# Exponential and sine tables in alternating order, exponent matmuls as row-tile pairs, constants as immediates

**Chip, cores, metric.** One Trainium2 chip, one core. The metric is the device time of one execution of the whole program in microseconds (us); medians over several runs are given. All runs told here are of the fast state.

## The reference

The program computes two independent things and sets them side by side: a segmented attention with memory (A) and a long convolution whose kernel K is a sum of complex exponentials (B). Only the making of K is touched here:

```python
dt = exp(log_dt)[:, None]
A, Bc, Cc = A_re + 1j*A_im, B_re + 1j*B_im, C_re + 1j*C_im
P = exp((dt*A)[:, :, None] * arange(L))          # D=1024, N=128, L=2048
K = einsum('dn,dnl,dn->dl', Cc, P, dt*Bc).real
...                                              # y = u convolved with K, by FFT
```

## The kernel before

B comes first, then A. B has a setup, then sixteen rounds that make tables of powers for K, then the spectra and inverse transforms. While the rounds run, A's projections of x ("pro"), the forward transforms of u ("ups", called the side matmuls here), and copies of weights are slipped in between. A itself, from 880 us on, streams weights from memory.

A round (sb) makes eight pairs of exponent matmuls (e = 0 to 7). TensorE writes the logarithm of the modulus (pa) and the angle in turns (pt); ScalarE (ACT) makes exp of the one (E) and rounds the other (kM); VectorE (DVE) takes the rounded turns off (nr); ACT makes sines (sn) and cosines (cs) of nr; DVE multiplies them by E; in the next round TensorE contracts them ("part", tile kp). Each engine takes up its work in the order of the program; the timeline under a_odd shows what that can cost, a wait of 3.20 us behind work of another kind.

```python
def exponents(pars, e):                       # four full-array matmuls, 128x328 each
    pa = ps_e.tile(...); pt = ps_t.tile(...)  # ps_e has one buffer, ps_t two
    for t_, q, Rs in ((pa, 0, (RG, RF)), (pt, 1, (RG, RN))):
        for f, R in enumerate(Rs):
            pe.matmul(t_[:, f, 0:8*NJ], lhsT=pars[q][:, e, :], rhs=R[...], start=True, stop=True)
    return pa, pt

for sb in range(17):
    npars = load_par(sb + 1)                  # four DMAs from GpSimd's queue
    for e in range(8):
        pa, pt = ex
        sc.activation(out=Es[..e], in_=pa, func=ACT.Exp)
        sc.activation(out=kM, in_=pt, func=ACT.Identity, bias=magic[:])
        v.scalar_tensor_tensor(out=nrs[..e], in0=kM, scalar=MAGIC, in1=pt, ...)
        ex = exponents(pars, e + 1)           # or of the next round
        if e == 0: v.tensor_tensor(out=ocs[1], in0=oE[1], in1=ocs[1], op=mult)
        if e % 2 == 1: part(osb, e // 2, ocs, osn)     # kp: 32 small matmuls + a DVE copy
        if e % 2 == 0: step_side()                     # ups: 8 matmuls + ACT copy or two DVE sums
    for i in range(2):
        sc.activation(out=sn[i], in_=nrs[i], func=ACT.Sin, scale=-TWO_PI)
        next(pro)
        v.tensor_scalar(nrs[i] = abs)
    next(pro)
    for i in range(2):
        sc.activation(out=cs[i], in_=nrs[i], func=ACT.Sin, scale=-TWO_PI, bias=hp[:])
        v.tensor_tensor(out=sn[i], in0=Es[i], in1=sn[i], op=mult)
        next(pro)
    v.tensor_tensor(out=cs[0], in0=Es[0], in1=cs[0], op=mult)
    next(pro); next(pro); next(mb)            # ... cut
```

kp and ups share two PSUM buffers in turn; what is still to be taken out of the older one is taken out when the next is asked for.

## Time and profile before

| | before |
|---|---|
| median, lowest, highest (first three runs) | 2541.84, 2531.63, 2552.6 us |
| profiled execution | 2562.5 us, mean clock 0.942 |
| the rounds | some 86 to 560 us |
| one round (mean of 14) | 29.0 us |

The lines behind this stand in the prediction. Read them so: an engine's busy share over the whole span says nothing about this change, since A takes two thirds of the time and is bound by DMA. What counts is one round, and in it who waits for whom.

### The profile page before, as it was taken

To read this page: it belongs to the slowest core of one execution; us is meant where nothing else is said; L and a number is where in the kernel's file an instruction comes from. 1 tells how busy PE (TensorE), PEld (TensorE's weight loads), DVE (VectorE), ACT (ScalarE), POOL (GpSimd) and SP (SyncE) were. 2 spreads that over 40 slices of the span, in tenths; PEclk is the share of its full clock that TensorE was granted. 3 is DMA by queue.
4 is the path that set the end of the run, shared out by engine and by line. 5 is a ranking of instruction groups with operands and counts; after the bars stand their busy time and mean duration, and the time that the engine had idled before them with its cause. 6 is when DMAs were issued, how large, how long until landed. Compare 5 with 4: busy or idle time off the path is not lost.

```text
span 2562.5 us, 76703 instructions
## 1 busy us (share of the span) xinstructions
PE 2055.3 (80%) x32856; PEld 1101.7 (43%) x32902; DVE 1498.0 (58%) x3224; ACT 1023.9 (40%) x1550; POOL 311.6 (12%) x601
## 2 busy tenths in 40 slices
PE   1588888857697778888888888888888888888879
PEld 1355555633242334444444444444444444444444
DVE  9687777879985245545454554545455454545450
ACT  6788788961121223323333332323333232333321
POOL 2133424442001100000000000000000000000020
PEclk6799999978898889999999999999999999999999
DMA  5665756543346999999999999999999999999992
GB/s 135 174 190 155 229 173 176 149 146 116 125 132 212 339 382 379 378 380 365 386 362 381 372 386 369 362 373 369 390 383 384 380 364 374 369 370 373 374 384 74
DMA packets 382387, 763.18 MB, mean 298 GB/s; under 512 B 118678, under 2 KB 210806, under 8 KB 379998
## 3 DMA queue, kind: packets, MB, share of 16 engines
q1 hardware_dynamic: 363006, 700.44, 76.1%
q0 software_dynamic: 14128, 39.99, 4.6%
q10 hardware_dynamic: 4912, 17.84, 2.0%
q8 instruction: 257, 4.21, 0.6%
q14 instruction: 84, 0.69, 0.1%
HBM read 703.35 MB, written 67.88 MB: 301 GB/s over the span
## 4 chain that ended last, share of the span: by engine, by line
DMA 33%; PE 28%; DVE 17%; ACT 9%; issue 8%; SPq 1%; POOL 0%; ACTq 0%; DVEq 0%; POOLq 0%
DMA wst<-WD_k 16%; PE acc L330 12%; DMA wst<-WD_o 10%; PE pp L429 3%; DMA wst<-WD_v 3%; PE pe L552 2%; ACT sn L1019 2%; PE pro L151 2%; PE tr L341 2%; ACT kM L994 1%; DVE piece L269 1%; PE ups L850 1%; ACT E L991 1%; PE pro L138 1%; ACT ev L336 1%
## 5 line engine op out<-in xcount | busy, mean ns | idle before, releaser
L330 PEld LDWEIGHTS <-hT 128*32 128x32 bf16 x12352 | 326.8, 97 | 474.1 <-issue 256.0
L330 PE MATMUL acc<-wst,hT 128*32 128x512 bf16 x3072 | 313.6, 393 | 163.3 <-DMA wst<-WD_k 67.4
L336 ACT CAST ev<-acc 128x512 bf16<-128x512 f32 x384 | 225.1, 586 | 414.4 <-PE acc L330 409.4
L429 PEld LDWEIGHTS <-oT 128*32 128x32 bf16 x8192 | 204.5, 97 | 116.6 <-issue 90.4
L269 DVE TENSOR_SCALAR piece<-keep 128x256 int32<-128x256 int32 (+1 forms) x640 | 191.4, 363 | 56.5 <-PE pp L429 31.1
L429 PE MATMUL pp<-W_o,oT 128*32 128x256 bf16 x5120 | 212.5, 277 | 6.8 <-DMA W_o<-in_A_Wo_dram 6.8
L330 PE MATMUL acc<-W_v,hT 128*32 128x512 bf16 x3072 | 211.1, 379 | 0.3 <-DMA W_v<-in_A_Wv_dram 0.3
L368 DVE TENSOR_REDUCE mx<-sc 128x8 f32<-128x320 f32 x128 | 62.4, 487 | 251.8 <-PE sc L361 251.6
L330 PE MATMUL acc<-W,hT 128*32 128x512 bf16 x2560 | 205.7, 392 | 0.0
L342 DVE COPY KT<-tr 128x512 bf16<-128x512 bf16 x64 | 27.2, 425 | 264.3 <-PE tr L341 264.3
L429 PE MATMUL pp<-wst,oT 128*32 128x256 bf16 x2560 | 129.2, 278 | 39.3 <-DMA wst<-WD_o 30.3
L342 ACT COPY QT<-tr 128x512 bf16<-128x512 bf16 x128 | 75.0, 586 | 192.6 <-PE tr L341 191.7
L1159 PE MATMUL yp<-Bt,mi 128*128 128x512 bf16 x379 | 115.5, 411 | 41.5 <-DMA mi<-MId 32.2
L416 ACT CAST oT<-pv 128x512 bf16<-128x512 f32 x128 | 75.1, 586 | 169.3 <-PE pv L402 166.9
L349 POOL COPY KT<-pk 128x128 bf16<-128x128 bf16 x128 | 37.6, 293 | 816.0 <-PE sc L361 454.4
L330 PE MATMUL acc<-W_q,hT 128*32 128x512 bf16 x1792 | 135.1, 383 | 0.0
L995 DVE SCALAR_TENSOR_TENSOR nr<-kM,ptt 128x656 f32<-128x656 f32 x128 | 104.9, 833 | 44.3 <-ACT kM L994 44.1
L151 PE MATMUL pro<-xTl,wsl 128*128 128x512 bf16 x493 | 116.6, 384 | 12.7 <-DVE kst L155 7.5
L370 ACT ACTIVATE sc<-sc 128x320 f32<-128x320 f32 x128 | 54.0, 422 | 154.8 <-DVE sc L369 148.0
L330 PE MATMUL acc<-W_k,hT 128*32 128x512 bf16 x1536 | 112.6, 401 | 0.0
L303 POOL COPY hT<-xt 128x192 bf16<-128x192 bf16 x64 | 22.2, 347 | 728.1 <-DMA xt<-XTd 442.0
L1075 PE MATMUL hps<-KT,MF 128*128 128x512 bf16 x374 | 93.3, 395 | 19.9 <-DVE x L1088 19.4
(288 smaller groups left out, 3766.7 us busy)
## 6 DMA issues: line engine op xcount, KB each, us to landing
wst<-WD_o SPq DMA_DIRECT2D x320, 512.0 KB
wst<-WD_k SPq DMA_DIRECT2D x256, 512.0 KB
wst<-WD_q SPq DMA_DIRECT2D x256, 512.0 KB
wst<-WD_v SPq DMA_DIRECT2D x256, 512.0 KB
Ud<-ux POOLq DMA_DIRECT2D x16, 1024.0 KB, 4.8
uq<-Ud SPq DMA_DIRECT2D x32, 512.0 KB
pk<-PKd SPq DMA_DIRECT2D x64, 192.0 KB
wsl<-in_A_Wk_dram SPq DMA_DIRECT2D x16, 512.0 KB
```

The lines of the kernel that those rows point to most:

```text
L151: nc.tensor.matmul(a[:], lhsT=w[:, kc, 128 * j:128 * j + 128], rhs=xTl[:, kc, :, :].rearrange("p s k -> p (s k)"), start=(kc == 0), stop=( ...
L269: nc.vector.tensor_scalar(out=out.bitcast(I32), in0=in_.bitcast(I32), scalar1=0, scalar2=None, op0=ALU.bitwise_or)
L330: nc.tensor.matmul(a[32 * g:32 * g + 32, o_:o_ + rhs.shape[1]], lhsT=hT[:, kc, :], rhs=rhs, start=(kc == 0), stop=(kc == KC - 1), tile_pos ...
L336: nc.scalar.copy(out=q[:], in_=a[:])
L342: eng(out=dst, in_=p[:, i, :, :, :])
L368: nc.vector.tensor_reduce(out=mx[:], in_=sc, axis=AX.X, op=ALU.max)
L370: nc.scalar.activation(out=sc, in_=sc, func=ACT.Exp, scale=scale)
L416: nc.scalar.copy(out=o[:], in_=p[:].rearrange("p a (g q) -> p a g q", g=4))
L429: nc.tensor.matmul(po[32 * qt:32 * qt + 32, :], lhsT=oT[:, h % 4, (h % 16) // 4, :], rhs=columns(w, 1024 * hh + 256 * qt, 256)[0][1], star ...
L995: v.scalar_tensor_tensor(out=nrs[e // 4][:, e % 4].rearrange("p f t j -> p f (t j)"), in0=kM[:], scalar=MAGIC, in1=ptv, op0=ALU.subtract, ...
L1075: pe.matmul(ps[:], lhsT=MF[:, 4 * rr + mc, cs, 128 * kc:128 * kc + 128], rhs=rhs, start=(i == 0 and mc == 0), stop=(i == 1 and mc == 3))
L1159: pe.matmul(yp[:], lhsT=m_[:, cs, kc, :], rhs=Bt[:, kc, half, j, c_, :], start=(n == 0), stop=(n == 15))
```

## The change

Its intent: Exp and Sin lie in different tables of ACT, so a round needs two table loads. If even rounds end with exponentials and odd rounds begin with them, half of the loads go. The exponent matmuls have two disjoint halves of rows, so two of them fit in the array at once as row tiles; for it the parameters are loaded twice, to both halves of the partitions. Constants pi/2 and MAGIC are given as immediates.

```diff
-def exponents(pars, e): ... four full-array matmuls
+    def rows_of(t_, par, R, e):
+        for f in range(2):
+            p = slice(64 * f, 64 * f + 64)
+            pe.matmul(t_[:, f, 0:8 * NJ], lhsT=par[p, e, :], rhs=R[p]..., start=True, stop=True, tile_position=(64 * f, 0))
+    def angles(pars, e):                      # ps_t
+    def exponents(pars, e, late_=False):      # ps_e, or ps_t in even rounds
-            for h in range(2):
-                gp.dma_start(out=par_t[sb % 2][q][24 * h:24 * h + 24],
+            for h, p0 in ((0, 0), (1, 24), (0, 64), (1, 88)):
+                gp.dma_start(out=par_t[sb % 2][q][p0:p0 + 24],
-  bias=hp[:] / bias=magic[:]
+  bias=HALF_PI / bias=MAGIC
 ...
+    for sb in range(0, 16, 2):
+        for e in range(8):                    # EVEN round: angles alone
+            fold(e, nrs, pt)                  # kM on ACT, nr on DVE
+            if e < 7: pt = angles(pars, e + 1)
+            if e == 0 and old is not None: scale(old[2], Es, 1)
+            if e % 2 == 1: old_part(e // 2)
+            if e % 2 == 0: step_side()
+        sines, with five of the round's seven projections
+        for e in range(8):                    # exponentials alone
+            power(e, Es, pa)
+            if e < 7: pa = exponents(pars, e + 1, True)
+            if e == 3: scale(sn, Es, 0); scale(cs, Es, 0)
+            if e in (2, 5): more()            # the other two projections
+        scale(sn, Es, 1); scale(cs, Es, 1)
+        sb += 1
+        for e in range(8):                    # ODD round: both, as before
+            power(e, Es, pa); fold(e, nrs, pt)
+            pa, pt = exponents(pars, e + 1), angles(pars, e + 1)
+            if e in (2, 4, 6, 7): old_part(...)        # before: e = 1, 3, 5, 7
+            if e % 2 == 0 ...: step_side()
+        sines as before, with all seven projections
```

More of the change, by code (lines that the diff above doesn't have):

```diff
@@ L597, in part_b @@
     make_identity(nc, ident[:])
-    hp = const.tile([128, 1], F32, name="hp")
-    v.memset(hp[:], HALF_PI)
-    magic = const.tile([128, 1], F32, name="magic")
-    v.memset(magic[:], MAGIC)
     ahead.open(ahead.ctx)
@@ L608, in part_b @@
     tabs = ctx1.enter_context(tc.tile_pool(name="b_tab", bufs=1))
-    RG = tabs.tile([128, 8, NJ], BF16, name="RG")
-    RF = tabs.tile([128, 8, NJ], BF16, name="RF")
-    RN = tabs.tile([128, 8, NJ], BF16, name="RN")
+    RE = tabs.tile([128, 8, NJ], BF16, name="RE")
+    RA = tabs.tile([128, 8, NJ], BF16, name="RA")
     par_t = [[tabs.tile([128, 8, 128], BF16, name="pt%d%d" % (q, n_)) for q in range(2)] for n_ in range(2)]
@@ L675, in matrices @@
                     v.tensor_scalar(out=tm[:].bitcast(I32), in0=tm[:].bitcast(I32), scalar1=0x7FFFFFFF, scalar2=None, op0=ALU.bitwise_and)
-                    sc.activation(out=MF[:, c - 4:c - 2, 0, :], in_=tm[:], func=ACT.Sin, scale=-TWO_PI, bias=hp[:])
+                    sc.activation(out=MF[:, c - 4:c - 2, 0, :], in_=tm[:], func=ACT.Sin, scale=-TWO_PI, bias=HALF_PI)
                 if 2 <= c < 18:
@@ L685, in matrices @@
                     kMs[c] = mg.tile([128, 2, 512], F32, name="mkM", tag="mkM")
-                    sc.activation(out=kMs[c][:], in_=tms[c][:], func=ACT.Identity, bias=magic[:])
+                    sc.activation(out=kMs[c][:], in_=tms[c][:], func=ACT.Identity, bias=MAGIC)
                 yield
@@ L707, in part_b @@
         pI = par.tile([128, 3], I32, name="pI")
-        gp.iota(pI[:, 0:1], pattern=[[1, 1]], base=0, channel_multiplier=1)
+        gp.iota(pI[:, 2:3], pattern=[[1, 1]], base=0, channel_multiplier=1)
+        v.tensor_scalar(out=pI[:, 0:1], in0=pI[:, 2:3], scalar1=63, scalar2=None, op0=ALU.bitwise_and)
         v.tensor_scalar(out=pI[:, 1:2], in0=pI[:, 0:1], scalar1=3, scalar2=None, op0=ALU.bitwise_and)
@@ L727, in part_b @@
         v.tensor_scalar(out=jF[:, 1, :], in0=jF[:, 1, :], scalar1=low[:], scalar2=pF[:, 2:3], op0=ALU.mult, op1=ALU.add)
-        for i, R in ((0, RG), (1, RF)):
-            v.tensor_tensor(out=R[:], in0=bcast_mid(own[:], NJ), in1=bcast_front(jF[:, i, :], 8), op=ALU.mult)
-        v.tensor_scalar(out=RN[:], in0=RF[:], scalar1=-1.0, scalar2=None, op0=ALU.mult)
+        v.tensor_copy(out=jF[0:64, 1, :], in_=jF[0:64, 0, :])
+        v.tensor_tensor(out=RE[:], in0=bcast_mid(own[:], NJ), in1=bcast_front(jF[:, 1, :], 8), op=ALU.mult)
+        v.tensor_copy(out=RA[0:64], in_=RE[0:64])
+        v.tensor_scalar(out=RA[64:128], in0=RE[64:128], scalar1=-1.0, scalar2=None, op0=ALU.mult)
         for ts in par_t:
@@ L924, in put_values @@
             put(Kd[640:641, dsl], kx[P0:P0 + 1, 40, :])
-    def exponents(pars, e):
-        pa = ps_e.tile([128, 2, 512], F32, name="pa", tag="pa")
-        pt = ps_t.tile([128, 2, 512], F32, name="ptt", tag="ptt")
-        for t_, q, Rs in ((pa, 0, (RG, RF)), (pt, 1, (RG, RN))):
-            for f, R in enumerate(Rs):
-                pe.matmul(t_[:, f, 0:8 * NJ], lhsT=pars[q][:, e, :], rhs=R[:].rearrange("p a b -> p (a b)"), start=True, stop=True)
-        return pa, pt
+    def rows_of(t_, par, R, e):
+        for f in range(2):
+            p = slice(64 * f, 64 * f + 64)
+            pe.matmul(t_[:, f, 0:8 * NJ], lhsT=par[p, e, :], rhs=R[p].rearrange("p a b -> p (a b)"), start=True, stop=True, tile_position=(64 * f, 0))
+        return t_
+    def angles(pars, e):
+        return rows_of(ps_t.tile([128, 2, 512], F32, name="ptt", tag="ptt"), pars[1], RA, e)
+    def exponents(pars, e, late_=False):
+        pool, tag = (ps_t, "ptt") if late_ else (ps_e, "pa")
+        return rows_of(pool.tile([128, 2, 512], F32, name="pa", tag=tag), pars[0], RE, e)
     def load_k(dh, qs, KT):
@@ L971, in load_u, with fold, power @@
         return us
+    flat = "p f t j -> p f (t j)"
+    def fold(e, nrs, pt):
+        ptv = pt[:, :, 0:8 * NJ]
+        kM = tmp.tile([128, 2, 8 * NJ], F32, name="kM", tag="kM")
+        sc.activation(out=kM[:], in_=ptv, func=ACT.Identity, bias=MAGIC)
+        v.scalar_tensor_tensor(out=nrs[e // 4][:, e % 4].rearrange(flat), in0=kM[:], scalar=MAGIC, in1=ptv, op0=ALU.subtract, op1=ALU.subtract)
+    def power(e, Es, pa):
+        sc.activation(out=Es[e // 4][:, e % 4], in_=pa[:, :, 0:8 * NJ].rearrange("p f (t j) -> p f t j", t=8), func=ACT.Exp)
@@ new lines, in scale, with sines @@
+    def scale(x, E, i):
+        v.tensor_tensor(out=x[i][:], in0=E[i][:], in1=x[i][:], op=ALU.mult)
+    def sines(nrs, sn, cs, after):
+        for i in range(2):
+            sc.activation(out=sn[i][:], in_=nrs[i][:], func=ACT.Sin, scale=-TWO_PI)
+            after()
+            v.tensor_scalar(out=nrs[i][:].bitcast(I32), in0=nrs[i][:].bitcast(I32), scalar1=0x7FFFFFFF, scalar2=None, op0=ALU.bitwise_and)
+        after()
+        for i in range(2):
+            sc.activation(out=cs[i][:], in_=nrs[i][:], func=ACT.Sin, scale=-TWO_PI, bias=HALF_PI)
+            yield i
+            after()
@@ L975, in part_b, with small_steps, shift_late, old_part @@
+    def small_steps():
+        next(mb, None)
+        for _ in range(2):
+            if copies:
+                copies.pop(0)()
+    def shift_late():
+        if late:
+            late.pop(0)()
+    def old_part(k):
+        if old is not None:
+            osb, osn, ocs = old
+            part(osb, k, ocs, osn)
+            if k == 3 and osb % 4 == 3:
+                put_values(osb)
+    def more(n=1):
+        for _ in range(n):
+            next(pro, None)
     pars = load_par(0)
     old = None
-    ex = exponents(pars, 0)
@@ L978, in part_b @@
-    for sb in range(17):
+    pt = angles(pars, 0)
+    for sb in range(0, 16, 2):
+        nrs = [tmp.tile(shg, F32, name="nr", tag="nr%d" % i, bufs=1) for i in range(2)]
+        npars = load_par(sb + 1)
+        for e in range(8):
+            fold(e, nrs, pt)
+            if e < 7:
+                pt = angles(pars, e + 1)
+            if e == 0 and old is not None:
+                scale(old[2], Es, 1)
+            if e % 2 == 1:
+                old_part(e // 2)
+            shift_late()
+            if e % 2 == 0:
+                step_side()
+        sn = [tmp.tile(shg, BF16, name="sn", tag="sn%d" % i, bufs=1) for i in range(2)]
+        cs = [tmp.tile(shg, BF16, name="cs", tag="cs%d" % i, bufs=1) for i in range(2)]
+        for i in sines(nrs, sn, cs, more):
+            pass
+        pa = exponents(pars, 0, True)
+        small_steps()
+        Es = [tmp.tile(shg, BF16, name="E", tag="E%d" % i, bufs=1) for i in range(2)]
+        for e in range(8):
+            power(e, Es, pa)
+            if e < 7:
+                pa = exponents(pars, e + 1, True)
+            if e == 3:
+                scale(sn, Es, 0)
+                scale(cs, Es, 0)
+            if e in (2, 5):
+                more()
+        pars = npars
+        pa, pt = exponents(pars, 0), angles(pars, 0)
+        scale(sn, Es, 1)
+        scale(cs, Es, 1)
+        old = (sb, sn, cs)
+        sb += 1
@@ L983, in part_b @@
             ks = [load_k(0, (sy,), ahead.pool.tile([128, 16, DH], BF16, name="KT", tag="kst"))]
-        if sb < 16:
-            nrs = [tmp.tile(shg, F32, name="nr", tag="nr%d" % i, bufs=1) for i in range(2)]
-            Es = [tmp.tile(shg, BF16, name="E", tag="E%d" % i, bufs=1) for i in range(2)]
+        nrs = [tmp.tile(shg, F32, name="nr", tag="nr%d" % i, bufs=1) for i in range(2)]
+        Es = [tmp.tile(shg, BF16, name="E", tag="E%d" % i, bufs=1) for i in range(2)]
         npars = load_par(sb + 1) if sb < 15 else None
         for e in range(8):
-            if sb < 16:
-                pa, pt = ex
-                sc.activation(out=Es[e // 4][:, e % 4], in_=pa[:, :, 0:8 * NJ].rearrange("p f (t j) -> p f t j", t=8), func=ACT.Exp)
-                ptv = pt[:, :, 0:8 * NJ]
-                kM = tmp.tile([128, 2, 8 * NJ], F32, name="kM", tag="kM")
-                sc.activation(out=kM[:], in_=ptv, func=ACT.Identity, bias=magic[:])
-                v.scalar_tensor_tensor(out=nrs[e // 4][:, e % 4].rearrange("p f t j -> p f (t j)"), in0=kM[:], scalar=MAGIC, in1=ptv,
-                                       op0=ALU.subtract, op1=ALU.subtract)
-                if e < 7:
-                    ex = exponents(pars, e + 1)
-                elif sb < 15:
-                    ex = exponents(npars, 0)
-            if old is not None:
-                osb, oE, osn, ocs = old
-                if e == 0:
-                    v.tensor_tensor(out=ocs[1][:], in0=oE[1][:], in1=ocs[1][:], op=ALU.mult)
-                if e % 2 == 1:
-                    part(osb, e // 2, ocs, osn)
-                if e == 7 and osb % 4 == 3:
-                    put_values(osb)
-            if late:
-                late.pop(0)()
+            power(e, Es, pa)
+            fold(e, nrs, pt)
+            if e < 7:
+                pa, pt = exponents(pars, e + 1), angles(pars, e + 1)
+            elif sb < 15:
+                pt = angles(npars, 0)
+            if e in (2, 4, 6, 7):
+                old_part(min(e // 2 - 1, 2) if e < 7 else 3)
+            shift_late()
             if e % 2 == 0 or (e == 7 and sb % 4 == 1):
                 step_side()
-        if sb == 16:
-            break
         pars = npars
@@ L1017, in part_b @@
         cs = [tmp.tile(shg, BF16, name="cs", tag="cs%d" % i, bufs=1) for i in range(2)]
-        for i in range(2):
-            sc.activation(out=sn[i][:], in_=nrs[i][:], func=ACT.Sin, scale=-TWO_PI)
-            next(pro, None)
-            v.tensor_scalar(out=nrs[i][:].bitcast(I32), in0=nrs[i][:].bitcast(I32), scalar1=0x7FFFFFFF, scalar2=None, op0=ALU.bitwise_and)
-        next(pro, None)
-        for i in range(2):
-            sc.activation(out=cs[i][:], in_=nrs[i][:], func=ACT.Sin, scale=-TWO_PI, bias=hp[:])
-            v.tensor_tensor(out=sn[i][:], in0=Es[i][:], in1=sn[i][:], op=ALU.mult)
-            next(pro, None)
-        v.tensor_tensor(out=cs[0][:], in0=Es[0][:], in1=cs[0][:], op=ALU.mult)
-        next(pro, None)
-        next(pro, None)
-        next(mb, None)
-        for _ in range(2):
-            if copies:
-                copies.pop(0)()
-        old = (sb, Es, sn, cs)
+        for i in sines(nrs, sn, cs, more):
+            scale(sn, Es, i)
+        scale(cs, Es, 0)
+        more(2)
+        small_steps()
+        old = (sb, sn, cs)
+    scale(old[2], Es, 1)
+    for k in range(4):
+        old_part(k)
+        shift_late()
+        step_side()
     for n_, f_ in enumerate(late):
```

## The prediction

> **What bounds the kernel now.** I read the page's slices first, then the sums by stretch of time, then the groups of the tables' stretch, then its chain, then one round's timeline.
>
> From the page: the busy tenths in 40 slices of 64 us each.
>
> ```profile
> PE   1588888857697778888888888888888888888879
> ...
> ACT  6788788961121223323333332323333232333321
> ...
> DMA  5665756543346999999999999999999999999992
> ```
>
> ACT is high only in the first nine slices, which hold the setup and the tables (from 86 us to some 560 us). From slice 14 on the DMA engines are full, and the chain there is weight transfers. The change touches only the first stretch, so whatever it wins or loses is a shift of some 475 us out of 2542.
>
> Sums by stretch, one for the fourteen rounds from the second to the fifteenth (the rounds begin at the load of the exponentials' table), columns in order length, PE, PEld, DVE, ACT, POOL, clock, DMA:
>
> ```profile
> 119.17:524.79 405.62, 339.07 (x3765) 225.06 (x3782) 316.14 (x383) 351.86 (x367) 159.89 (x229) 0.95 0.65 184
> ```
>
> A round is 405.62/14 = 29.0 us. ACT works 351.86/14 = 25.1 of it (87%), PE 24.2 and DVE 22.6. No engine is full; three nearly full ones hand work to each other in strict order. The groups of that stretch on ACT (busy us, mean ns, then idle before and its releasers):
>
> ```profile
> L994 ACT ACTIVATE kM<-ptt,magic 128x656 f32<-128x656 f32 x112 | 91.0, 812 | 0.4 <-PE ptt L931 0.4
> L991 ACT ACTIVATE E<-pa 128x656 bf16<-128x656 f32 x112 | 80.8, 722 | 13.2 <-PE pa L931 9.8 <-DVE cs L1027 1.9
> L1024 ACT ACTIVATE cs<-nr,hp 128x2624 bf16<-128x2624 f32 x28 | 68.4, 2477 | 0.2 <-DVE nr L1021 0.2
> L1019 ACT ACTIVATE sn<-nr 128x2624 bf16<-128x2624 f32 x28 | 66.1, 2387 | 0.2
> L991 ACT ACT_TABLE_LOAD x15 | 19.2, 1283 | 0.3
> L1019 ACT ACT_TABLE_LOAD x14 | 18.0, 1283 | 0.2
> L855 ACT COPY ua<-ups 128x512 f32<-128x512 f32 x28 | 16.5, 588 | 18.1 <-PE ups L850 18.1
> L155 ACT CAST kst<-pro 128x512 bf16<-128x512 f32 x18 | 10.4, 576 | 12.5 <-PE pro L151 12.5
> L143 ACT CAST vst<-pro 128x512 bf16<-128x512 f32 x12 | 7.0, 580 | 8.7 <-PE pro L138 8.7
> ```
>
> Every round loads two tables, 2.57 us, and ACT's idle time, 53.8 us or 3.84 a round, is nearly all waits for PE: side matmuls (ups), projections (pro), exponents (pa). The chain of this stretch says the same: it changes hands all the time, no engine has half of it.
>
> ```profile
> by line: ACT sn L1019 11.0%; PE pro L151 10.6%; issue 10.2%; ACT kM L994 7.1%; PE ups L850 6.8%; PE pro L138 6.2%; ACT E L991 6.2%; DVE nr L995 5.8%; DVE us L859 3.6%; DVE us L858 3.4%; DVE nr L1021 3.2%; ACT L991 2.8%; DVE cs L1004 2.8%; D
> ```
>
> **What the Trainium skill says.** (1) "ScalarE: Activation LUTs", section "What ACT_TABLE_LOAD costs": a switch is a load of about 1283 ns plus a drain of about 1380 ns. The trace agrees on the load, 1283 ns each time; the drain isn't there to save: at 254.12 the load begins 0.02 us after the copy before it, and the sine at 255.41 follows it at once. I count 1.283 us a load. (2) The same section: a per-partition pointer operand adds about 93 ns to an ACTIVATE. The trace agrees: the cosines with hp take 2477 ns, the sines without it 2387, 90 ns apart. (3) "TensorE: Matmul & The Clock Gate", section "The mechanism" of Part 3: matmuls in different row groups start some 4 ns apart and run together. No run of this kernel shows it, since it has no row tiles. (4) "TensorEngine Tiling (Array Packing)", section "Key Properties": changing the tiling mode drains TensorE. The trace agrees roughly: in the timeline of PE, exponent matmuls start 0.14 us apart, but the first column-tiled kp matmul starts 0.23 us after the last of them (250.21 to 250.44), so a switch costs about 0.09 us.
>
> **The change part by part.**
>
> *Table loads.* Now each round goes exponentials, sines. Afterwards an even round goes angles, sines, exponentials and the odd one exponentials, sines, so the table at the seam is already there. 16 of 32 loads go: 16 x 1.283 = 20.5 us of ACT, 2.57 us for a pair of rounds.
>
> *Constants in the instructions.* Each round has 8 kM and 2 cosines with a pointer: 10 x 0.09 = 0.9 us a round, 1.8 a pair. The setup has 16 more, 1.4 us, but there ACT waits for DVE and for DMA; nothing counted.
>
> *Exponent matmuls as row tiles.* Four matmuls of 0.14 us each (start to start) for a step e, 0.55 us; as two pairs 0.28 us plus a switch into the mode and out of it, 0.18 us if both pairs stand together (odd rounds), 0.36 if alone (even). So PE wins 0.55 - 0.46 = 0.1 us a step in odd rounds and about nothing in even ones. I expect PE's busy time to fall by far more (each of four records of 302 ns is halved or overlaps), with little in the end time.
>
> *Parameter loads.* 8 POOL issues a round for 4, of 0.567 us: 2.3 us more on an engine busy 11.4 of 29 us; hidden. At the start the first fold waits for the last of them: some 2 x 0.55 = 1.1 us later.
>
> *Order.* Removed and added DVE work is equal. What changes is where it stands. I follow ACT through a pair, in durations from the timeline less their overlap (kM 0.62 without the pointer, E 0.62, sine 2.30, copy 0.50). ACT's work for a pair: 2 x 25.13 - 2.57 - 1.8 = 45.9 us. To it comes its idle time, 2 x 3.84 = 7.7 us before. Afterwards:
> - Even round, angles: ACT has 8 x 0.62 + 2 x 0.50 = 6.0 us, but DVE has 8 folds of 0.77, a product of 1.44, 4 kp copies of 0.42 and 4 us sums of 0.60: 11.6 us. ACT may leave about 3 us before DVE's end (the first sine needs only the first half of nr). Idle 11.6 - 6.0 - 3.0 = 2.6.
> - Even round, sines: 5 projections on PE (8 x 0.22 = 1.76 us each) beside 9.2 us of ACT: casts wait less than before, 0.8 instead of 1.5.
> - Even round, exponentials: after each of two projections placed among them the next exponent matmul comes 1.76 us late, against 0.62 for which ACT has work: 2 x 1.2 = 2.4.
> - Odd round, both: before, a step with side matmuls alternated with a step with kp; now e = 2, 4, 6 have both, 0.6 + 1.0 us on PE, with pa in one buffer, and the PSUM buffer of the side matmuls comes free one step later. I put 1.5 for it, estimated from one wait of some 2 us a round less what is saved in ua's waits.
> - Odd round, sines, still 7 projections, 12.3 us of PE against 11.7 of ACT: 1.5 as before.
>
> Idle 2.6 + 0.8 + 2.4 + 1.5 + 1.5 = 8.8. A pair becomes 45.9 + 8.8 = 54.7 us against 2 x 28.97 = 57.9: 3.2 us less, times 8 pairs = 26 us; 1 us comes back at the start. 2541.8 - 26 + 1 = 2517. I take **2516 us**, 1.0% less. From the tables' end on all is the same work, DMA bound, and only moves forward.
>
> **The rivals.**
> - *PE and ACT were both on the chain, and both savings count.* For it: 23.6% of the chain is PE's three side groups, and ACT waits for PE. With idle time shrinking to 5 us a pair the gain would be (57.9 - 50.9) x 8 = 56 us, 2486. Against it: the projections and side matmuls, which ACT waits for, are not touched, and mode switches eat the pairs' gain. Only this passes 2%.
> - *DVE becomes the bound.* Even rounds put 11.6 us of DVE beside 6.0 of ACT. If DVE's end, with no overlap by the first sine, sets the angles' part, and its four products after the exponentials (2.9 us late) also hold the odd round's folds, add some 3 us a pair: gain near zero, 2540.
> - *The table loads were hidden anyway.* In rounds where PE's projections ran late (5.42 and 10.67 us long pieces in the chain at 170.81 and 285.48), ACT had time for the load. Then only half of the 20.5 us counts: gain 16 us, 2526.
> - *A later start of transfers.* The weights' copies and K's stores hang on rounds, the same number a round; a shorter stage shifts them. A chance collision like the 4.50 us on PVd<-vst at 300 us is worth 5 to 10 us either way.
>
> **Range and chances.** Between the rivals 2486 and 2540 lie 54 us; the three runs of before alone spread over 21 us. I give 2490 to 2540 eight chances in ten. 2% is 51 us, under 2491: only the first rival whole reaches it, 0.12. Slower by 2% would need 3.2 us more a round, which no part of the change adds: 0.02. Within 2%: 0.86.
>
> **What would show each step.** Table loads: 16 or 17 in place of 32, 1283 ns each. kM at some 715 to 725 ns in place of 812, the cosines at 2390. Pairs: two exponent matmuls that start within a few ns of each other, with a gap of about 0.1 us at each change of mode. Order: DVE with hardly a pause in the even round's angles while ACT waits for it there; gaps in ACT of over 1 us behind the projections among the even round's exponentials; PE ups waiting for DVE's us in odd rounds. Setup: the first fold about 1 us later than 94.7. The weights' stretch unchanged in length. I am wrong if a pair of rounds takes under 52 us (then waits for PE vanished which I kept), or over 57 (then DVE or the projections hold the new order).

## The result

The changed kernel took 2627.32 us (2621.79 to 2629.92, 4 runs) against 2545.66 us (4 runs) of the kernel before: ratio 1.0336, 95% interval 1.0296 to 1.0376. It is 3.4% slower, some 82 us, where 26 us less was forecast. Ratios here and below are those on record, from the fast runs of the same rounds; they are not quite the ratio of the medians (1.0321 here), and the two ways differ by up to 0.2% in the runs below.

The page of the changed kernel, the slices (66 us each); PEclk is the granted clock of TensorE in tenths:

```profile
PE   1487887875779678888888888888888888888888
...
ACT  6666667675112122332333323323333233233231
...
PEclk6687878886989889999999999999999999999999
DMA  5655585354333799999999999999999999999992
```

The tables' stretch is a slice longer, ACT is emptier in it (6s where 7s and 8s were), and the clock there lies at 7 and 8 tenths in many slices. In the page of before these slices read:

```profile
PEclk6799999978898889999999999999999999999999
```

After the stretch the program is the same: from the last round's sines to the end, 625.7 to 2628.1 us, 2002 us pass, in the kernel before 2017 (545.6 to 2562.5). I take these 15 us as scatter: in the profiles of all runs told here the remainder takes 1991 to 2017 us, and the profiled execution of the kernel before was 17 us above the median. The tables themselves scatter less: two profiles of the changed kernel end them at 625.7 and 620.8 us, two of the version with doubled pairs at 609.0 and 608.4. So the start of the last round's sines, called the tables' end, is given below beside the time of each run; it is one profile, good to some 5 us. The change moved it by 80.1 us.

ACT's groups between 130 and 626 us of the changed kernel, to be laid beside those in the prediction:

```profile
L982 ACT ACTIVATE kM<-ptt 128x656 f32<-128x656 f32 x120 | 86.5, 724 | 45.9 <-PE ptt L926 43.5 <-DVE KxT L899 1.5 <-DVE us L856 0.3
L986 ACT ACTIVATE E<-pa 128x656 bf16<-128x656 f32 x120 | 82.2, 723 | 55.1 <-PE pa L926 50.4 <-DVE cs L989 4.6
L999 ACT ACTIVATE cs<-nr 128x2624 bf16<-128x2624 f32 x28 | 65.8, 2387 | 0.2 <-DVE nr L996 0.2
...
L994 ACT ACT_TABLE_LOAD x8 | 10.3, 1283 | 0.1
L986 ACT ACT_TABLE_LOAD x7 | 9.0, 1283 | 0.1
```

What was to be saved is saved: kM takes 724 ns for 812, the cosines 2387 for 2477, fifteen loads for 29 in nearly the same count of rounds. But the waits before kM and E, 13.6 us together in fourteen rounds before (19.0 in fifteen), are 101 us in fifteen.

The sums over the phases of seven pairs of rounds, as stretches of the timeline bounded by ACT's first instruction of each phase (the mixed loop by its first kM, so that its first exponential, 0.6 us, stands in the phase before). Of the changed kernel, in this order: even round's angles, its sines (with the table load after them), its exponentials, odd round's mixed loop, its sines:

```profile
sum 96.90, PE 78.24 PEld 51.72 DVE 86.16 ACT 46.39 POOL 57.42; mean PE 11.18 PEld 7.39 DVE 12.31 ACT 6.63 POOL 8.20
...
sum 85.53, PE 61.71 PEld 36.93 DVE 49.31 ACT 79.04 POOL 39.60; mean PE 8.82 PEld 5.28 DVE 7.04 ACT 11.29 POOL 5.66
...
sum 71.89, PE 46.69 PEld 21.08 DVE 33.08 ACT 41.86 POOL 17.39; mean PE 6.67 PEld 3.01 DVE 4.73 ACT 5.98 POOL 2.48
...
sum 133.58, PE 99.54 PEld 59.78 DVE 88.02 ACT 83.58 POOL 77.01; mean PE 14.22 PEld 8.54 DVE 12.57 ACT 11.94 POOL 11.00
...
sum 89.40, PE 84.48 PEld 51.35 DVE 66.09 ACT 73.97 POOL 12.76; mean PE 12.07 PEld 7.34 DVE 9.44 ACT 10.57 POOL 1.82
```

Each first number divided by seven is the length of a phase. Beside the prediction's terms (us for a pair of rounds):

| phase | length | ACT busy | ACT idle | idle predicted |
|---|---|---|---|---|
| even, angles | 13.84 | 6.63 | 7.2 | 2.6 |
| even, sines | 12.22 | 11.29 | 0.9 | 0.8 |
| even, exponentials | 10.27 | 5.98 | 4.3 | 2.4 |
| odd, mixed loop | 19.08 | 11.94 | 7.1 | 1.5 |
| odd, sines | 12.77 | 10.57 | 2.2 | 1.5 |
| pair | 68.2 | 46.4 | 21.8 | 8.8 |

ACT's work was forecast at 45.9 us and came to 46.4. The whole error lies in its idle time. Against 57.9 us a pair before, a pair is 10.3 us longer, and eight pairs are the 82 us.

### The profile page after: what moved, and what is told of

Same layout as the page of the kernel before. It is cut to its first block, busy times and chain, and to the rows that moved or that the text cites. A ratio compares the mean times of both kernels' runs of the same rounds, so it can differ in the third digit from the quotient of the medians.

```text
span 2628.1 us, 76787 instructions
## 1 busy us (share of the span) xinstructions
PE 2083.6 (79%) x32855; PEld 1093.7 (42%) x32902; DVE 1499.2 (57%) x3224; ACT 991.1 (38%) x1534; POOL 352.7 (13%) x665
## 4 chain that ended last, share of the span: by engine, by line
PE 32%; DMA 31%; DVE 15%; issue 12%; ACT 8%; POOL 2%; SPq 1%; ACTq 0%; DVEq 0%; POOLq 0%
DMA wst<-WD_k 14%; PE acc L330 12%; DMA wst<-WD_o 10%; PE pp L429 3%; PE pro L151 3%; PE ups L847 3%; DMA wst<-WD_v 2%; PE pe L552 2%; PE pro L138 2%; PE tr L341 2%; DMA wst<-WD_q 2%; DVE nr L983 1%; DVE piece L269 1%; ACT E L986 1%; ACT cs L999 1%
## 5 line engine op out<-in xcount | busy, mean ns | idle before, releaser
L151 PE MATMUL pro<-xTl,wsl 128*128 128x512 bf16 x492 | 123.3, 401 | 9.6 <-DVE kst L155 6.1
L982 ACT ACTIVATE kM<-ptt 128x656 f32<-128x656 f32 x128 | 92.0, 724 | 62.3 <-PE ptt L926 58.9
L1139 PE MATMUL hps<-KT,MF 128*128 128x512 bf16 x374 | 96.3, 404 | 18.5 <-DVE x L1152 17.9
```

The lines of the kernel that those rows point to most:

```text
L151: nc.tensor.matmul(a[:], lhsT=w[:, kc, 128 * j:128 * j + 128], rhs=xTl[:, kc, :, :].rearrange("p s k -> p (s k)"), start=(kc == 0), stop=( ...
L982: sc.activation(out=kM[:], in_=ptv, func=ACT.Identity, bias=MAGIC)
L1139: pe.matmul(ps[:], lhsT=MF[:, 4 * rr + mc, cs, 128 * kc:128 * kc + 128], rhs=rhs, start=(i == 0 and mc == 0), stop=(i == 1 and mc == 3))
```

## The experiments

Names with b_ are the kernel before with something of the change put in; names with a_ are the changed kernel with something put back. "Before" is always the kernel before on the same chip. The tables' end is 545.6 us in the kernel before and 625.7 in the changed one.

| run | what differs | median us | ratio to before (95% interval) | tables' end, us |
|---|---|---|---|---|
| b_const | constants as immediates | 2545.21 | 0.9986 (0.9968 to 1.0004) | 540.2 |
| b_noload | no table switches (wrong on purpose) | 2529.0 | 0.9936 (0.9918 to 0.9954) | 529.4 |
| b_rows | row tiles, doubled loads | 2563.62 | 1.0070 (1.0052 to 1.0089) | 554.7 |
| b_loads | doubled loads alone | 2566.04 | 1.0075 (1.0042 to 1.0107) | 557.4 |
| b_order | kp at even e | 2586.81 | 1.0169 (1.0122 to 1.0217) | 588.2 |
| b_const_sp | immediates, loads from SyncE | 2562.95 | 1.0083 (1.0054 to 1.0111) | 556.1 |
| a_full_odd_pro | three parts undone | 2568.05 | 1.0097 (1.0059 to 1.0135) | 570.0 |
| a_full_odd | two undone | 2586.89 | 1.0155 (1.0134 to 1.0175) | 586.5 |
| a_odd_pro | two undone | 2585.35 | 1.0159 (1.0119 to 1.0199) | 577.7 |
| a_odd | kp back at odd e | 2597.56 | 1.0199 (1.0169 to 1.0230) | 591.3 |
| a_full | full-array matmuls, four loads | 2605.57 | 1.0221 (1.0190 to 1.0252) | 602.7 |
| a_odd_pro_side | a_odd_pro, side steps moved | 2619.3 | 1.0288 (1.0261 to 1.0316) | 608.8 |
| a_full_loads | full-array matmuls, eight loads | 2622.64 | 1.0302 (1.0261 to 1.0343) | 607.6 |
| a_twice | each pair issued twice | 2625.78 | 1.0307 (1.0283 to 1.0330) | 609.0 |
| a_twice_again | the same | 2617.72 | 1.0285 (1.0243 to 1.0328) | 608.4 |
| a_again | the changed kernel | 2636.38 | 1.0373 (1.0344 to 1.0403) | 620.8 |

All but b_noload gave right results. After the result three theories stood: (A) row tiles keep the array active for less time, the granted clock falls, and everything on TensorE takes longer; (B) the odd rounds' order, kp beside the side matmuls, makes ACT wait; (C) the projections among the even round's exponentials hold them up. Later came (D): the split of an even round is itself a loss, since DVE is full in one part and idle in the other.

### Each part by itself in the kernel before, and undone in the changed one

**b_const**

```diff
-bias=hp[:]  /  bias=magic[:]
+bias=HALF_PI  /  bias=MAGIC
```

> The kernel before with its constants (pi/2 and the rounding constant) as immediates, nothing else. All theories: kM and the cosines lose 0.09 us each, so the time falls by some 5 to 15 us (0.2 to 0.6%), the clock of the tables' stretch stays near 0.94.

Measured: 0.14% less, some 3.5 us, and the interval includes no change. kM fell to 714 ns, the cosines to 2386. ACT's work fell by 0.9 us a round, but the mixed loop only from 15.36 to 15.09 us and the sines from 13.52 to 13.48: two thirds went back into waits, for TensorE above all. In the profile the tables end 5.4 us earlier, 1.8 of which stem from the setup (the first kM at 93.0 us, for 94.7).

**b_rows**

```diff
-    pe.matmul(t_[:, f, ...], lhsT=pars[q][:, e, :], rhs=RG/RF/RN)                # 128 rows
+    pe.matmul(t_[:, f, ...], lhsT=pars[q][p, e, :], rhs=R[p], tile_position=(64 * f, 0))
     (and the eight parameter loads)
```

> The kernel before with its exponent matmuls as pairs of row tiles (and the eight parameter loads that they need), in the order of before. Theory A (the granted clock falls because the array is active for half the time): mean clock of the exponentials' halves falls from 0.94 to under 0.85, the side matmuls in them take 1.9 us instead of 1.05 in many places, and the time rises by 20 to 60 us. Theory B (the order of the odd rounds) and theory C (projections among the exponentials): clock as before, time within 10 us of before or up to 15 us less.

Measured: 0.7% slower, 18 us, with the clock of the mixed loops at 0.92 after 0.95. The time lies between the ranges of the theories, and the clock that theory A asked for didn't come: in the order of before, row tiles alone hardly lower it. With the doubled loads alone the loss is as large (b_loads, below).

**a_full**

```diff
-row-tile pairs, eight parameter loads a round
+four full-array matmuls, four parameter loads a round, as in the kernel before
```

> The changed kernel with its exponent matmuls as four full-array matmuls again (zeros kept), all else as changed. Theory A: the clock of the tables' stretch goes back to 0.92 or more and the time to 2530 to 2565 us. Theories B and C: clock may rise a little, the time stays at 2600 or more.

Measured: 2605.57 us, ratio 1.0221, so the time is where theories B and C had it. The clock is where theory A had it: in the odd rounds' mixed loop it went from 0.65 to 0.95, and the loop from 19.1 to 17.9 us. Most of the loss stayed. And this edit undid two things, tiles and loads.

**a_odd**

```diff
-            if e in (2, 4, 6, 7):
-                old_part(min(e // 2 - 1, 2) if e < 7 else 3)
+            if e % 2 == 1:
+                old_part(e // 2)
```

> The changed kernel with the four kp groups of the odd rounds back at e = 1, 3, 5, 7 (alternating with the side matmuls). Theory B: the waits of ACT for pa and ua in the odd rounds' first half go, 19 us of it become under 16, the time falls by 25 us or more, to 2600 or less. Theory A: the clock stays under 0.88 in the stretch and the time falls by less than 20 us.

Measured: 2597.56 us, as theory B has it; the odd rounds' mixed loop fell from 19.1 to 15.0 us. The clock in it rose from 0.65 to 0.83 with the row tiles still there: TensorE waits less and is busy for 12.3 of the loop's 15.0 us, for 14.2 of 19.1 in the changed kernel.

Here is such a wait in the changed kernel, an odd round of it. TensorE's timeline (kp's short matmuls left out):

```profile
273.81 0.32 PE L926 MATMUL ptt<-RA,pt 64*128 64x328 bf16 x2 [0.29 <-DVE nr L983]
...
276.25 1.87 PE L847 MATMUL ups<-u_h,MF 128*128 128x256 bf16 x8 [1.51 <-DVE us L856]
278.05 0.45 PE L926 MATMUL pa<-RE,pt 64*128 64x328 bf16 x2
```

and DVE and ACT in the same time:

```profile
274.16 0.84 DVE L983 SCALAR_TENSOR_TENSOR nr<-kM,ptt 128x656 f32<-128x656 f32 x1 [0.41 <-ACT kM L982]
...
274.92 0.68 DVE L855 TENSOR_TENSOR us<-ua,ups 128x512 f32<-128x512 f32 x1
275.51 0.68 DVE L856 TENSOR_TENSOR us<-ua,ups 128x512 f32<-128x512 f32 x1
...
278.55 0.72 ACT L986 ACTIVATE E<-pa 128x656 bf16<-128x656 f32 x1 [3.20 <-PE pa L926]
```

Read backwards: E stands 3.20 us still because its pa comes only after eight side matmuls; they began at 276.25, when DVE had emptied their PSUM buffer (us); DVE could do that only after the fold nr of this step. In the order of before, kp at the odd step in between asks for the emptying one step earlier. And the eight side matmuls take 1.87 us here; at the full clock they take 1.03 to 1.05.

### Do they add, and what is left

**a_full_odd**

```diff
 a_full and a_odd together
```

> The changed kernel with both undone: full-array exponent matmuls, and kp at e = 1, 3, 5, 7 in odd rounds. If the clock and the odd rounds' order are separate losses, their gains add: about 22 + 30 us less than the changed kernel, 2575 us. If both cure the same waits, 2590 us. Theory D (splitting an even round into folds alone and exponentials alone is itself the loss, since DVE is full in the one and idle in the other): even so it stays over 2560 us, the even rounds' folds still take over 13 us.

Measured: 2586.89 us, ratio 1.0155. Undone one at a time the two won 1.15% and 1.37%; together 1.81%. Part of the gain is the same. That the low clock stretches the very waits that the order makes would explain it; no run tests this further. The even rounds' angles still take 14.1 us.

**a_odd_pro**

```diff
+        pa = exponents(pars, 0, True)        # ahead of the sines
         for i in sines(nrs, sn, cs, more): pass
-        pa = exponents(pars, 0, True)
+        more(2)
 ...
-            if e in (2, 5):
-                more()
```

(with a_odd's edit)

> The changed kernel with kp at e = 1, 3, 5, 7 in odd rounds, and with the two projections taken from among the even round's exponentials into its sines (first exponent matmul issued ahead of them). Theory C (the projections hold the exponentials): the exponentials fall from 9.8 us to under 7.5, the sines grow by less than that, and the time falls 10 to 20 us below that of the kernel with the order alone (2597.6). If the projections only move the wait: within 6 us of 2597.6.

Measured: 2585.35 us, 12 us below a_odd. The exponentials fell from 9.76 to 7.50 us, just at the border that was set for theory C, the sines grew from 12.97 to 14.39. So theory C holds in its direction, and the tables end 13.6 us earlier. Two things limit it: the two intervals (1.0119 to 1.0199 and 1.0169 to 1.0230) overlap, and of what a pair of rounds won, some 1.7 us, more than half lies in the odd round's mixed loop, which fell from 15.0 to 13.9 us and of which theory C says nothing.

**a_odd_pro_side**

```diff
-            if e % 2 == 0:
-                step_side()                  # in the even round's angles
+            if e % 2 == 0:
+                step_side()                  # in its exponentials
```

(with a_odd_pro's edits)

> The same, and the even round's four side matmul steps moved from among its folds to among its exponentials, where DVE is idle. Theory D: the folds fall from 13.9 us to 11 or less, the exponentials grow by under 1.5 us, the time falls by 10 to 20 us against the same kernel without this move. If DVE is not what sets the folds (PE or the seam with the odd round is): less than 6 us.

Measured: 2619.3 us, 34 us slower than a_odd_pro, outside both forecasts. The sums over the angles of seven even rounds, a_odd_pro's first, then those of this run:

```profile
sum 97.89, PE 77.90 PEld 51.63 DVE 86.02 ACT 46.31 POOL 58.03; mean PE 11.13 PEld 7.38 DVE 12.29 ACT 6.62 POOL 8.29
```

```profile
sum 82.75, PE 51.73 PEld 33.80 DVE 69.97 ACT 39.18 POOL 42.45; mean PE 7.39 PEld 4.83 DVE 10.00 ACT 5.60 POOL 6.07
```

The angles' part follows DVE: 13.98 us long with 12.29 of DVE, 11.82 with 10.00, each time 1.7 to 1.8 us more than DVE's work. So far theory D, though the angles stayed above the 11 us that it asked for. But the exponentials grew from 7.5 to 11.4 us and the odd round's mixed loop from 13.9 to 16.2: the side matmuls now stand in the way there. Moving work out of the full phase isn't free, since it comes with TensorE work that others queue behind.

**a_full_odd_pro**

```diff
 a_full, a_odd and the projections' move together: only the alternation and the immediates are left
```

> The changed kernel with all three undone (full-array matmuls, kp at odd e, no projections among exponentials): what is left is the alternation of the rounds and the constants. If the alternation itself costs (folds bound by DVE, exponentials with DVE idle): still 20 to 40 us slower than before, 2568 to 2586. If the three were the whole loss: 2520 to 2550.

Measured: 2568.05 us, ratio 1.0097, inside the forecast of "the alternation itself costs". An odd round takes 26.8 us here (14.28 + 12.53; 27.4 with its first exponential) against 29.0 before, so it does win much of what it was made for; an even round takes 35.0 (14.15 + 13.49 + 7.39).

**b_order**

```diff
-                if e % 2 == 1:
-                    part(osb, e // 2, ocs, osn)
+                if e in (2, 4, 6, 7):
+                    part(osb, min(e // 2 - 1, 2) if e < 7 else 3, ocs, osn)
```

> The kernel before with kp at e = 2, 4, 6, 7 (together with the side matmuls) instead of e = 1, 3, 5, 7, nothing else. Theory B: the mixed loop grows by 1 to 3 us a round by ACT's waits for pa and ua, the time rises by 15 to 50 us. If the order hurts only at the low clock of the row tiles: within 10 us of before.

Measured: 2586.81 us, 1.69% slower, some 43 us, at a clock of 0.92 in the mixed loops. That is theory B without any help of row tiles: the mixed loop grew from 15.36 to 18.22 us. ACT's groups between 119 and 588 us of b_order:

```profile
L994 ACT ACTIVATE kM<-ptt,magic 128x656 f32<-128x656 f32 x120 | 97.2, 810 | 7.9 <-PE ptt L931 7.9
L991 ACT ACTIVATE E<-pa 128x656 bf16<-128x656 f32 x120 | 86.6, 722 | 57.7 <-PE pa L931 54.5 <-DVE cs L1027 1.9
```

In the kernel before, between 119 and 545 us, also fifteen rounds:

```profile
L991 ACT ACTIVATE E<-pa 128x656 bf16<-128x656 f32 x120 | 86.6, 722 | 18.6 <-PE pa L931 15.1 <-DVE cs L1027 1.9
```

The wait for pa is 54.5 us in fifteen rounds, where it was 15.1.

### What the loads, of tables and of parameters, are worth

**b_noload**

```diff
-sc.activation(out=Es[...], in_=pa, func=ACT.Exp)
+sc.activation(out=Es[...], in_=pa, func=ACT.Identity)      # wrong on purpose
```

> The kernel before with Identity in place of Exp, so that no table is ever switched in the rounds (wrong result on purpose). It shows what all 32 loads (41 us of ACT) are worth in the order of before. If the loads lie on the path, as the prediction has it: 30 to 45 us less, 2505 to 2515 us. If waits for PE take their place: under 20 us less.

Measured: 2529.0 us, 0.64% or 16 us less. All 32 table loads are 32 x 1.283 = 41 us of ACT, and taking every one of them away wins 16. ACT's groups between 119 and 529 us of this run:

```profile
L991 ACT ACTIVATE E<-pa 128x656 bf16<-128x656 f32 x119 | 86.0, 723 | 28.9 <-PE pa L931 16.9 <-DVE cs L1027 10.3
L994 ACT ACTIVATE kM<-ptt,magic 128x656 f32<-128x656 f32 x120 | 97.5, 812 | 0.0
...
L155 ACT CAST kst<-pro 128x512 bf16<-128x512 f32 x18 | 10.4, 577 | 17.0 <-PE pro L151 17.0
```

Before E, ACT now waits for DVE's products (10.3 us, for 1.9) and somewhat longer for pa (16.9 us, for 15.1 in as many rounds) and for pro. If the half of the loads that the change removes is worth half of this, it is some 8 us; that half alone was not run.

**b_loads**

```diff
-            for h in range(2):
-                gp.dma_start(out=par_t[sb % 2][q][24 * h:24 * h + 24],
+            for h, p0 in ((0, 0), (1, 24), (0, 64), (1, 88)):
+                gp.dma_start(out=par_t[sb % 2][q][p0:p0 + 24],
```

(the added rows meet zero factors, so the result is right)

> The kernel before with the eight parameter loads a round of the change (the second copies go to rows whose factors are zero, the result stays right). If the loss of the row tiles in the order of before (18 us) comes from the loads: 10 to 20 us slower than before. If from the row tiles: within 6 us of before.

Measured: 0.75% slower, 19 us, as much as b_rows with its tiles. The timeline of this run at the end of a round:

```profile
339.65 2.71 POOL L882 DMA_DIRECT2D pt<-PB  x5
...
345.75 0.30 PE L931 MATMUL pa<-RG,pt 128*128 128x328 bf16 x1 [1.62 <-DMA pt<-PB]
...
347.17 0.43 PE L931 MATMUL ptt<-RG,pt 128*128 128x328 bf16 x1 [0.99 <-DMA pt<-PB]
```

GpSimd, which also issues K's stores and adds spectra, comes to the loads for the next round only late in this one (335.2 to 342.4 us), and TensorE's exponent matmuls wait for them with all that is queued behind them. This is the worst case and not the rule: from the second round to the last such waits of TensorE add up to 2.8 us. At the start the first kM comes at 96.9 us, for 94.7. The tables' end is 11.8 us later than before, so these two explain some 5 us of it; the rest was not followed wait by wait, and why the whole time grew by 19 us is not shown.

**b_const_sp**

```diff
-                gp.dma_start(out=par_t[...])
+                sy.dma_start(out=par_t[...])        # and immediates
```

> The kernel before with constants as immediates and with its four parameter loads issued by SyncE in place of GpSimd. If the loads cost by the GpSimd queue that they share with K's stores: 5 to 15 us less than before, 2530 to 2540. If SyncE's queue, which waits for the projections, holds them as long: within 5 us, or slower by up to 20.

Measured: 0.83% slower. SyncE's queue, which also waits for projections (157 us for their matmuls between 80 and 570 us), is no better place. No version tried that gives right results is clearly faster than the kernel before; b_const comes nearest.

### The clock

**a_twice**

```diff
-        for f in range(2):
+        for f in (0, 1, 0, 1):               # the second pair writes the same values again
```

> The changed kernel with every pair of row-tile matmuls issued twice (the second writes the same values). Theory A (clock follows the array's activity): mean clock of the odd rounds' first half goes up from 0.65 to over 0.8, and the time falls by 5 to 25 us although PE has more to do. If changes of tiling mode or the row tiles as such lower the clock: it stays under 0.72 and the time rises by 5 to 20 us.

Measured: the clock of the odd rounds' mixed loop rose from 0.65 to 0.97, as theory A has it, and the loop fell from 19.1 to 17.5 us. The time, 2625.78 us, was within noise of the changed kernel's, while the tables' end came 16.7 us earlier. So the clock's cause was settled and its price in time not.

**a_full_loads, a_again, a_twice_again** (one chip, one call; a_full_loads has full-array matmuls and keeps the eight loads)

> The changed kernel with four full-array exponent matmuls, but with its eight parameter loads kept. Against the changed kernel it differs in the row tiles alone, against a_full in the loads alone. If the 22 us that a_full won were the clock: 2600 to 2608 us here. If they were the loads: 2618 to 2630 us, with a clock near 0.95 in the odd rounds' first half all the same.

> The changed kernel itself once more, on the same chip: 2620 to 2632 us.

> The doubled pairs once more, beside the changed kernel on the same chip. If the restored clock is worth time: 5 to 20 us less than a_again. If the second pair takes back what the clock gives: within 5 us.

Measured: ratios 1.0302, 1.0373, 1.0285. The changed kernel itself came out 0.4% slower than at first, a little above what I gave it. The doubled pairs are 0.9% below it on this chip (0.3% in the first comparison), full-array matmuls with all eight loads 0.7% below. Both keep what else the change has, so the clock is worth between 0.3 and 0.9%, 7 to 22 us. The tables' ends narrow this: against a_again they come 12.4 us (doubled pairs) and 13.2 us (full-array) earlier, against the first profile of the changed kernel 17 to 18. By the whole times the loads are the rest of what a_full won: 1.0302 to 1.0221, 0.8% or 21 us, which agrees with b_loads. By the profiles they are far less: the tables of a_full_loads end 4.9 us after those of a_full, and the first kM is already 3.6 us later (96.9 and 93.3). Where the other 16 us come from is open. One mixed loop of the same odd round, as sums of a stretch (length, then busy time of PE, PEld, DVE, ACT, POOL, then clock): the changed kernel,

```profile
269.76:290.52 20.76, 15.30 (x193) 9.28 (x193) 13.02 (x18) 12.03 (x19) 11.66 (x19) 0.62 0.10 24
```

full-array matmuls with eight loads,

```profile
264.70:282.48 17.78, 12.43 (x199) 9.12 (x199) 13.00 (x18) 12.10 (x20) 10.87 (x18) 1.00 0.12 28
```

and doubled pairs:

```profile
266.76:284.80 18.04, 12.93 (x229) 8.89 (x229) 13.03 (x18) 12.14 (x20) 10.84 (x18) 1.00 0.12 28
```

DVE and ACT do the same in all three. TensorE is busy for 15.30 us at clock 0.62 and for 12.93 at clock 1.00 although it then issues every pair twice.

## Why the prediction was wrong, step by step

**Right:** the table loads and the pointer operands. Counts and durations came as forecast, ACT's work for a pair to 0.5 us, and A's part of the program only moved. Pairs do run together, the two matmuls of a pair starting 5 ns apart (median of 256 pairs): in the changed kernel,

```profile
342.02 0.32 PE L926 MATMUL pa<-RE,pt 64*128 64x328 bf16 x2 [1.17 <-ACT E L986]
342.16 0.32 PE L926 MATMUL ptt<-RA,pt 64*128 64x328 bf16 x2
342.41 1.05 PE L847 MATMUL ups<-u_h,MF 128*128 128x256 bf16 x8
```

two matmuls as a pair take 0.32 us where one takes 0.30, the next pair follows 0.14 us later, and the side matmuls 0.25 us after that, so a change of mode costs 0.11 us, near the 0.09 of the estimate. The late start was 1.4 us, forecast 1.1, but by luck: the doubled loads alone delay the first kM by 2.2 us (b_loads), and the immediates, for whose work in the setup nothing was counted, alone bring it forward by 1.8 (b_const).

**Wrong.** The step that failed is the sum of ACT's idle time: "2.6 + 0.8 + 2.4 + 1.5 + 1.5 = 8.8" us a pair of rounds, where 21.8 were measured. The prediction held that no part of the change adds 3.2 us a round; it added 5.1. Its own sign of being wrong, a pair over 57 us, came true with 68.2: DVE and the projections do hold the new order, but the order of the odd rounds and the clock add about as much. The ladder a_full_odd_pro, a_full_odd, a_full, a_full_loads, a_again gives the sizes: 1.0097, 1.0155, 1.0221, 1.0302, 1.0373. At 25.5 us a per cent the steps are 25, 15, 17, 21 and 18 us. (With the first timing of the changed kernel, 1.0336, the last step is 9.) The tables' ends along the same ladder, from 545.6 us before, give 24, 17, 16, 5 and 13 us (18 with the first profile of the changed kernel). The two ladders agree except on the fourth step, the loads.

1. *"Idle 11.6 - 6.0 - 3.0 = 2.6", the even round's angles.* It was 7.2. The 3 us by which ACT was to leave before DVE's end were not there: the phase is DVE's 12.3 us and 1.5 more. In all seven even rounds the first sine begins just 0.3 to 0.4 us before the last fold ends. ACT's own last kM ends only 0.6 to 1.6 us before that sine, and in three of the rounds the sine waits another 0.6 us for the last kp of the round before. The rival "DVE becomes the bound" was the right one here; it was sized at 3 us a pair and is 4.6. In a_full_odd_pro, where all else is undone, a pair takes 62.1 us for the predicted 54.7, and the angles, 14.15 us long with 6.7 of ACT's work, are 4.9 of these 7.4.
2. *"Parameter loads ... hidden".* Whole times put them at about 20 us, alone in the kernel before and alone in the changed one; the profiles show 11.8 and 4.9 us of that in the tables. GpSimd's spare time was counted as an average of a round; in b_loads it got to the loads too late for TensorE at least once, and the start is later by two to four us. So the step failed, but its cause is only in part known.
3. *"I put 1.5 for it", the odd round's order.* The wait that I described is there, but it is 7.1 us a round with the low clock. The order alone costs 43 us in the kernel before (sixteen rounds; 41 by the medians), 17 us of the changed one at full clock (eight rounds, a_full against a_full_odd), and with the row tiles, where it also lowers the clock, 35 to 44 us (a_odd against the two timings of the changed kernel).
4. *The clock, which no step mentions.* I halved the array's active time and looked at nothing but its queue. In the mixed loops of odd rounds the granted clock fell to 0.65, and the eight side matmuls took 1.87 us for 1.05. Neither row tiles alone (b_rows, 0.92) nor the order alone (b_order, 0.92) does that; both together do. Doubled pairs, which add nothing but activity, bring it back to 0.97.
5. *"2 x 1.2 = 2.4", projections among the exponentials.* Measured 4.3 of idle time, partly at a lowered clock (0.76 in this phase); 12 to 15 us in all.
6. *The gain, 2.57 and 1.8 us a pair at full value.* The rival "the table loads were hidden anyway" was nearer: all 32 loads are worth 16 us of 41, the immediates 3.5 of 14, by an interval that includes no gain at all.

What stays open: what the doubled loads cost beyond the few us that the profiles show in the tables; a_odd_pro_side's loss is located (exponentials and the odd loop) but not tested further; and the steps of the ladder are 9 to 25 us each with intervals of 5 to 10 us either way on each rung, and they don't add exactly when taken in another order.

## What to carry to other kernels

Where three engines hand work to each other at 78 to 87% each, as here, a saving on one of them can mostly turn into waits (25 us of 41 for the table loads): measure its worth by taking the whole cost away once, even with a wrong result, before rebuilding the order for it. A loop that mixes the kinds of work spreads the load of every engine; splitting it by kind made one part here as long as DVE's work in it and 1.5 us more, while ACT was busy for half of it. When matmuls are made cheaper in a stretch where TensorE often waits, look at the granted clock there, and at the order in which others queue behind the same PSUM buffers.

## What the Trainium skill lacked or had wrong

- "ScalarE: Activation LUTs", section "What ACT_TABLE_LOAD costs": a switch is given as 1283 ns and about 1380 ns of drain, 2.66 us in total. The load is 1283 ns here; no drain shows as idle time beside it (0.02 us before it, the sine at once after it). The figure for a pointer operand held (812 to 724 ns, 2477 to 2387).
- "TensorE: Matmul & The Clock Gate", section "Why this matters for your kernels": the advice is to leave no pauses of TensorE over some 3 us. In the changed kernel's odd rounds no pause between its matmuls' records exceeded 1.6 us (2.1 in its second profile, a_again), and the mean clock was 0.65; the same loops with pairs issued twice, with pauses up to 3.7 us, had 0.97. So the advice doesn't suffice here. The page's section on short idling between groups of matmuls does tell of a clock that swings without long pauses; that making the matmuls shorter, as row tiles do, can bring this about isn't said.
- No page that I read has a figure for a change of tiling mode; here it cost 0.09 to 0.11 us.
